# A fused attention and two-MLP kernel: a renewed cost list and a new table of places for the planned order

## The chip, the cores and the metric

The kernel runs on one core of a Trainium2 chip. The metric is the device time of one execution in microseconds (us), from the median of a few runs. A core has five engines that run side by side and meet only through semaphores: TensorE (PE in the profile; its weight loads are PEld), VectorE (DVE), ScalarE (ACT), GpSimd (POOL) and SyncE (SP), which here issues nearly all DMAs.

## The reference, cut to what matters

```python
def _attn_ref(q, k, v, g_q, g_k):            # q, k, v: 4 batches x 12 heads x 448 x 64
    q_n, k_n = rmsnorm(q, g_q), rmsnorm(k, g_k)
    scores = scale * np.matmul(q_n, k_n.transpose(0, 1, 3, 2))
    attn = softmax(scores)                   # with the row maximum taken off
    return np.matmul(attn, v)
x = attn_out.transpose(0, 2, 1, 3).reshape(1792, 768)
def _moe_ref(x, w_in, w_out, g_ln):          # 768 -> 1024 -> 768
    h = x @ w_in
    return layernorm(h * softmax(h)) * g_ln @ w_out
def _moe2_ref(x, w_in, w_out):               # 768 -> 2048 -> 768
    h = x @ w_in
    return (h - np.tanh(h)) @ w_out
```

## The kernel before

The work falls into three parts. Attention runs over 24 pairs of heads, numbered 0 to 23. For a pair the rows of `k` and `q` are loaded (`qk`), normalised (`qn`, on GpSimd from the third pair on), and transposed on TensorE (`qkps`, 4 + 4 small matmuls). ScalarE and VectorE split the result into a high and a low part (`wk`, `wq`), and DMAs on SP's queue spread these over the buffers `k0` to `k2` and `q0` to `q2` ("q<-wq", "k<-wk"). Seven matmuls (`mps`) then give scores whose row maxima VectorE takes (`nm`); a transpose (`nmps`), a copy on ScalarE (`nt`) and a 2 KB DMA ("q<-nt") put the maxima into the `q` buffer, so that the second scores (`sps`, 16 matmuls for a pair) come out with the maximum already taken off. ScalarE takes the exponential (`pf`), and eight matmuls with the values (`pvps`) make the output, which goes through DRAM (`xd`).

The first MLP works on four blocks of tokens and lies between the pairs of the later batches: `hps` (first product), `lps` (transposes of the normalised `hb`), `x2ps` (second product). Its weights are 8-byte numbers in memory: a raw block is loaded (`raw`), turned into floats by a chain on GpSimd or ScalarE and VectorE (`val`), split (`w`), saved to DRAM and read again for later blocks ("w<-w_in", "w<-w_out"). The last block's first product (`moe_h_last`, `hps` with 512 columns) and the second MLP (`h2ps`, `ops`) come last.

What sets the order: a `Recorder` takes down every operation of attention and of the first three blocks' stages with what it depends on, and `place` then simulates the engines. `cost` gives the time that an operation holds its engine and how much later its result is there; `transfer` that of a DMA's data. At each step the earliest engine takes, among the operations that could start, the one with the smallest place: its number in the recording (`op.at`) plus a shift by kind (`op.late`), which `SHIFT` names, for instance "qkps tensor" for transposes on TensorE or "raw load" for loads from the kernel's inputs. `can` says from when an operation may start with regard to buffers. `slack` and `doubt` are added to what comes from another engine and from a DMA, and `ahead` is how long before its first user's start a load may be issued. Where the simulated TensorE would idle, `fill` puts matmuls on a constant tile (`idle<-still`, called fillers below) into the order. The result is issued as it stands, so each engine works through its list in order and waits on semaphores where the simulation was too hopeful. What is recorded after `rec.give()` (the last block's stage and the second MLP) is ordered by the framework, not by this planner.

All operations are issued from one helper, so that the profile puts nearly everything on L203 (L204 in the changed kernel); rows are told apart by their tiles.

Of the kernel before, what the change touches and what calls it, by code (L numbers as in the profile page):

```python
# [167 lines left out]
def _real(x):  # L168
# [1 line left out]


SHIFT = {
    "bs vector": 288, "e scalar": 299, "gln scalar": 64, "gps tensor": -190, "grow vector": 30, "hb scalar": 8,
    "hb vector": 158, "hps tensor": -30, "k scalar": 355, "k vector": -282, "mps tensor": -35, "mv vector": 34,
    "nmps tensor": -256, "nr scalar": 31, "nr vector": -3, "nt scalar": 3, "ones vector": 47, "pf scalar": -23,
    "pvps tensor": 100, "q gpsimd": 9, "q scalar": -94, "q vector": 391, "qd scalar": 405, "qd vector": -111,
    "qk load": -26, "qkps tensor": -1088, "qn gpsimd": 38, "qn vector": -7, "raw load": -69, "rr scalar": 36,
    "rr vector": -247, "rs gpsimd": 6, "rs vector": 91, "sps tensor": -77, "ss vector": 66, "sx scalar": 46,
    "sx vector": -33, "va gpsimd": 84, "va load": -55, "val scalar": -18, "val vector": -10, "w gpsimd": -85,
    "w scalar": 352, "w sync": -115, "w vector": 466, "w_in_ sync": -148, "w_out_ sync": 47, "wk scalar": -155,  # L180
    "wk vector": -42, "wq vector": 123, "x scalar": -55, "x2ps tensor": 314, "xd sync": 13, "xo scalar": -69,
    "xo vector": -16, "xs scalar": 359, "xu vector": -308, "zero vector": -400,
}


class Recorder:
# [51 lines left out]
    def cost(self, op):  # L238
        n = 1
        for d in (op.out.shape if isinstance(op.out, View) else [1, 1])[1:]:  # L240
            n *= d
        src = next((x for x in op.ins if isinstance(x, View)), None)
        m = n
        if src is not None:
            m = 1
            for d in src.shape[1:]:
                m *= d
        big = max(n, m)
        if op.queue == "tensor":
            if op.what == "transpose":  # L250
                return (0.095 if n < 128 else 0.108), 0.2
            rhs = op.kw["rhs"]
            if rhs.root.dtype != F32:
                return 0.0025 + n * 0.000451, 0.2
            return (0.475 if rhs.p1 - rhs.p0 == 64 else 0.75), 0.2
        if op.eng == "dma":
            inside = all(isinstance(x, View) and not x.root.far for x in (op.out, op.ins[0]))
            return (0.62 if inside else 0.46), 0.0
        if op.queue == "scalar":
            t = 0.15 + 0.000875 * big  # L260
            if n <= 64:
                t += 0.045
            t += 0.09 * sum(isinstance(op.kw.get(x), View) for x in ("bias", "scale"))
            if "accum_out" in op.kw:
                t += 0.2
            return t, 0.034
        if op.queue == "gpsimd":
            if op.what == "memset":
                return 0.5, 0.034
            if n == 1:  # L270
                return 0.67, 0.034
            if op.what == "tensor_copy":
                return 0.6, 0.034
            if op.what == "tensor_scalar":
                return 1.6, 0.034
            return (0.25 + 0.0022 * n if op.out.p1 - op.out.p0 == 128 else 1.135), 0.034
        if op.what == "memset":
            return 0.06, 0.034
        if op.what == "tensor_scalar" and n >= 64:
            return 0.2 + 0.00054 * n, 0.034  # L280
        if big <= 16:
            return 0.18, 0.034
        slow = isinstance(src, View) and src.dims and abs(src.dims[-1][0]) > 1
        return 0.156 + 0.00103 * big + (0.1 if slow else 0.0), 0.034

    @staticmethod
    def transfer(op):
        v = op.out if isinstance(op.out, View) else op.ins[0]
        o = next((x for x in op.ins if isinstance(x, View)), v)
        run, size = None, 1  # L290
        for x in (v, o):
            r = 1
            for stride, k in reversed(x.dims):
                if k == 1:
                    continue
                if stride != r:
                    break
                r *= k
            run = r if run is None else min(run, r)
        for d in v.shape:  # L300
            size *= d
        run = 4 * min(run, 512 if len(v.shape) == 4 and v.shape[-1] == 2 else 1024)
        packets = -(-4 * size // run)
        if run < 64:
            return 0.025 * packets
        return max(1, packets / 16.0) * (8 + 0.05 * run) * 1e-3
# [11 lines left out]
    def place(self):  # L318
# [23 lines left out]
        feeds = [[] for _ in ops]  # L342
        for op in ops:
            if op.queue == "tensor":
                r = op.out.root
                for d, o in op.deps.items():
                    if r not in o.refs:
                        r.wait += 1
                        feeds[d].append(r)
            else:  # L350
                for r in op.refs:
                    if r.psum:
                        r.into += [x for x in op.refs if x is not r and x.tile_ is None and not x.psum and x not in r.into]
        opened = dict.fromkeys(queue, 0)
# [8 lines left out]

        def can(op):
            t = op.ready
            for r in op.refs:
                if r.tile_ is not None or r.open:
                    continue
                s = slots[r.key]
                if not s:  # L370
                    return None
                if opened[r.line] != r.turn or r.wait:
                    return None
                t = max(t, r.from_)
                for x in r.into:
                    if not x.open and len(slots[x.key]) < x.turn - opened[x.line] + 1:
                        return None
                if r.psum and r.rank and key_limit.get(r.pool.name, 0) >= len(s):
                    return None
                t = max(t, min(s))  # L380
            return t

        key_limit = self.reserve
# [1 line left out]
        while placed < total:  # L385
# [33 lines left out]
            if op.eng == "dma":  # L419
# [1 line left out]
                    start = max(start, lanes[-8])  # L421
                free[e] = start + took
                wire = max(free[e] + 0.4, wire) + self.transfer(op)
                done = wire + 1.3
                lanes.append(max(done, lanes[-1] if lanes else 0.0))
            else:
                free[e] = start + took
                done = free[e] + late
            op.start, op.done = start, done
            ready[e].remove(op)  # L430
            order.append(op)
# [11 lines left out]
            for u in users[op.at]:  # L443
# [2 lines left out]
                    slack = self.slack[u.rank] + (self.doubt if op.eng == "dma" else 0.0)  # L446
                    u.ready = max(u.ready, done + self.notice.get(u.queue, 0.0) + slack)
                else:
                    u.ready = max(u.ready, start + took)
                if u.left == 0:  # L450
                    ready[u.queue].append(u)
        return order
# [20 lines left out]
    notice = {"tensor": 0.02, "gpsimd": 0.045}  # L473
    lag = 0
    warm = 9.0
    passes, ahead = 2, 12.0
    slack, doubt = (0.0, 0.6), 0.6
    still = None

    def give(self):  # L480
# [888 lines left out]
```

## Time and profile before

| | us |
|---|---|
| median of 3 runs | 1104.23 |
| lowest and highest | 1103.9, 1302.5 |
| the profiled execution | 1106.91 |
| its span, first to last instruction | 1104.9 |
| PE busy in the span | 1075.6 |
| of that in fillers | 50.57 |
| DVE, ACT, POOL busy | 704.2, 495.8, 231.5 |

The profiled execution's own time stands 2.0 us above its span, and 2.7 us above the median. Busy time of PE counts fillers too, and a matmul's recorded length overlaps the next one's, so a busy PE is not yet one that does useful work all the time.

### The profile page before, as it was taken

To read this page: it belongs to the slowest core of one execution; us is meant where nothing else is said; L and a number is where in the kernel's file an instruction comes from. 1 tells how busy PE (TensorE), PEld (TensorE's weight loads), DVE (VectorE), ACT (ScalarE), POOL (GpSimd) and SP (SyncE) were. 2 spreads that over 40 slices of the span, in tenths; PEclk is the share of its full clock that TensorE was granted. 3 is DMA by queue.
4 is the path that set the end of the run, shared out by engine and by line. 5 is a ranking of instruction groups with operands and counts; after the bars stand their busy time and mean duration, and the time that the engine had idled before them with its cause. 6 is when DMAs were issued, how large, how long until landed. Compare 5 with 4: busy or idle time off the path is not lost.

```text
span 1104.9 us, 15904 instructions
## 1 busy us (share of the span) xinstructions
PE 1075.6 (97%) x5716; PEld 906.2 (82%) x5716; DVE 704.2 (64%) x1312; ACT 495.8 (45%) x996; POOL 231.5 (21%) x204
## 2 busy tenths in 40 slices
PE   8898999999999899999899999999999999999998
PEld 7565677757777779779699989899999999998998
DVE  8786767878878843545664057375767666675444
ACT  5675767878667564574154154322212121212110
POOL 2222132302001210003300034242314241422000
PEclk9998999999999999999899999999999999999999
DMA  6886988986999998558586442021111111110004
GB/s 168 201 216 156 255 223 258 255 194 161 277 287 290 309 259 218 185 168 265 171 280 211 152 161 87 32 68 47 58 39 58 58 58 58 58 58 1 1 29 171
DMA packets 112470, 171.21 MB, mean 155 GB/s; under 512 B 30656, under 2 KB 78216, under 8 KB 112392
## 3 DMA queue, kind: packets, MB, share of 16 engines
q1 hardware_dynamic: 112368, 170.20, 53.5%
q8 instruction: 45, 0.74, 0.3%
q14 instruction: 33, 0.27, 0.1%
q10 hardware_dynamic: 24, 0.01, 0.0%
HBM read 109.32 MB, written 29.10 MB: 125 GB/s over the span
## 4 chain that ended last, share of the span: by engine, by line
PE 78%; DMA 10%; DVE 6%; ACT 4%; issue 2%; POOL 1%; SPq 0%; DVEq 0%; ACTq 0%; POOLq 0%
PE ops L203 21%; PE h2ps L203 21%; PE pvps L203 9%; PE x2ps L203 8%; PE hps L203 8%; PE sps L203 5%; PE mps L203 3%; PE idle L203 2%; DMA q<-wq 2%; DVE val L203 2%; DMA w_out<-w 1%; DMA q<-nt 1%; DMA raw<-in_moe_w_out_dram 1%; DMA xr<-xd 1%; PE qkps L203 1%
## 5 line engine op out<-in xcount | busy, mean ns | idle before, releaser
L203 PE MATMUL ops<-w,gT 128*128 128x384 f32 x1344 | 257.6, 336 | 0.0
L203 PE MATMUL h2ps<-x2s,w 128*128 128x512 f32 (+1 forms) x1152 | 256.5, 365 | 0.0
L203 PEld LDWEIGHTS ops<-w,gT 128*128 128x128 f32 x1344 | 235.8, 188 | 8.3
L203 PEld LDWEIGHTS h2ps<-x2s,w 128*128 128x128 f32 x1152 | 200.4, 188 | 27.6
L203 DVE SCALAR_TENSOR_TENSOR val<-raw,val 128x512 int32<-128x512 int32 (+1 forms) x192 | 149.2, 779 | 66.8 <-POOL val L203 63.5
L203 DVE TENSOR_TENSOR ob<-ops,ob 128x384 f32<-128x384 f32 x196 | 108.4, 553 | 102.4 <-PE ops L203 101.9
L203 PE MATMUL pvps<-pf,va 128*128 128x448 f32 (+1 forms) x384 | 172.4, 574 | 0.0
L203 POOL TENSOR_TENSOR w<-val,w 128x512 fp32r<-128x512 f32 x60 | 81.0, 1352 | 389.4 <-ACT w L203 387.0
L203 PE MATMUL sps<-q,k 128*128 128x448 f32 (+3 forms) x400 | 140.1, 457 | 6.2 <-DMA q<-nt 3.7
L203 DVE TENSOR_REDUCE nm<-mps 128x1 f32<-128x448 f32 x168 | 99.4, 618 | 62.2 <-PE mps L203 61.8
L203 PE MATMUL hps<-w,xs 128*128 128x256 f32 (+1 forms) x828 | 132.5, 314 | 4.8 <-ACT hb L203 4.2
L203 PEld LDWEIGHTS hps<-w,xs 128*128 128x128 f32 x828 | 118.1, 193 | 16.2 <-ACT hb L203 4.6
L203 PE MATMUL x2ps<-lnT,w 128*128 128x384 f32 (+1 forms) x720 | 125.3, 329 | 0.3 <-DVE lnT L203 0.3
L203 PEld LDWEIGHTS x2ps<-lnT,w 128*128 128x128 f32 x720 | 117.4, 189 | 5.2 <-issue 3.9
L203 ACT ACTIVATE th<-h2ps 128x512 f32<-128x512 f32 (+1 forms) x64 | 34.8, 544 | 179.6 <-PE h2ps L203 155.7
L203 ACT ACTIVATE pf<-sps 128x448 f32<-128x448 f32 (+1 forms) x169 | 89.1, 539 | 52.7 <-PE sps L203 50.4
L203 PEld LDWEIGHTS sps<-q,k 128*128 128x128 f32 (+3 forms) x400 | 69.6, 186 | 51.8 <-issue 28.1
L203 PEld LDWEIGHTS pvps<-pf,va 128*128 128x128 f32 (+1 forms) x384 | 64.0, 194 | 34.0 <-issue 24.7
L203 POOL TENSOR_SCALAR val<-raw 128x512 f32<-128x512 f32 x48 | 79.0, 1646 | 36.5 <-DVE w L203 17.7
L203 ACT ACTIVATE gT<-th 128x512 fp32r<-128x512 f32 (+1 forms) x64 | 37.1, 579 | 99.1 <-PE ops L203 66.8
L203 POOL TENSOR_TENSOR qn<-qk,rr 112x512 f32<-112x512 f32 x44 | 47.0, 1087 | 144.2 <-DVE rr L203 56.4
L203 DVE TENSOR_TENSOR th<-h2ps,th 128x512 f32<-128x512 f32 (+1 forms) x64 | 39.7, 621 | 44.0 <-ACT th L203 43.9
(95 smaller groups left out, 1036.6 us busy)
## 6 DMA issues: line engine op xcount, KB each, us to landing
w<-w_out SPq DMA_DIRECT2D x48, 512.0 KB
raw<-in_moe_w_in_dram SPq DMA_DIRECT2D x36, 512.0 KB
raw<-in_moe_w_out_dram SPq DMA_DIRECT2D x36, 512.0 KB
w<-w_in SPq DMA_DIRECT2D x24, 512.0 KB
k<-wk SPq DMA_DIRECT2D x46, 224.0 KB
q<-wq SPq DMA_DIRECT2D x46, 224.0 KB
w_in<-w SPq DMA_DIRECT2D x12, 512.0 KB
w_out<-w SPq DMA_DIRECT2D x12, 512.0 KB
```

What stands on the lines that cost most here:

```text
L203: return f(*[_real(x) for x in a], **{n: _real(x) for n, x in kw.items()})
```

## The change

Three things change, all inside the planner. No operation of the computation is added, removed or altered, and the number of instructions on DVE, ACT, POOL and SP stays the same.

The cost list is renewed: a DMA takes SP 0.5, 0.66 or 0.7 us instead of 0.46 or 0.62; its data lands 2.0 us after the wire is done instead of 1.3; a full-precision matmul over 64 rows holds PE 0.58 instead of 0.475 us; VectorE, ScalarE and GpSimd are free 0.08, 0.08 and 0.05 us before an operation ends (`overlap`), but an operation of the same engine that needs the result waits for its end and the delay behind it. The margins are other ones: `slack` by rank (attention, MLP stage) from (0.0, 0.6) to (0.07, 0.18), `doubt` from 0.6 to 0.44, `ahead` from 12 to 185.2 us. The rule for buffers (`can`) now counts an operation that opens several buffers of one kind, and a PSUM buffer waits for the inputs of every matmul that touches it. And the table of places is new in nearly all its entries.

```diff
 SHIFT = {
...
-    "qk load": -26, "qkps tensor": -1088, "qn gpsimd": 38, "qn vector": -7, "raw load": -69, "rr scalar": 36,
+    "nt scalar": -1395, "ones vector": -357, "pf scalar": -1312, "pvps tensor": 76, "q gpsimd": -80, "q scalar": -59,
...
-            return (0.475 if rhs.p1 - rhs.p0 == 64 else 0.75), 0.2
+            return (0.58 if rhs.p1 - rhs.p0 == 64 else 0.75), 0.2
...
-            return (0.62 if inside else 0.46), 0.0
+            return (0.7 if inside else 0.66 if self.run(op)[0] <= 64 else 0.5), 0.0
...
-                r = op.out.root
-                for d, o in op.deps.items():
-                    if r not in o.refs:
-                        r.wait += 1
-                        feeds[d].append(r)
+                for r in op.refs:
+                    for d, o in op.deps.items():
+                        if r.psum and r not in o.refs:
+                            r.wait += 1
+                            feeds[d].append(r)
...
-                if not s:
+                n, m = new.get(r.key, 0), lines.get(r.line, 0)
+                new[r.key], lines[r.line] = n + 1, m + 1
+                if len(s) <= n:
                     return None
-                if opened[r.line] != r.turn or r.wait:
+                if opened[r.line] + m != r.turn or r.wait:
                     return None
...
-                t = max(t, min(s))
+                t = max(t, sorted(s)[n])
...
-                done = wire + 1.3
+                done = wire + 2.0
...
-                free[e] = start + took
-                done = free[e] + late
+                free[e] = start + took - self.overlap.get(e, 0.0)
+                done = start + took + late
...
-                    u.ready = max(u.ready, start + took)
+                    u.ready = max(u.ready, start + took + (0.0 if e == "tensor" else late))
...
-    passes, ahead = 2, 12.0
-    slack, doubt = (0.0, 0.6), 0.6
+    passes, ahead = 2, 185.2
+    overlap = {"vector": 0.08, "scalar": 0.08, "gpsimd": 0.05}
+    slack, doubt = (0.07, 0.18), 0.44
```

What it makes of the order on PE: every matmul of the computation is still there, as often as before, and the rows from the end of the last block's first product to the program's end are the same ones. The fillers go from 183 to 88. Up to the first `pvps` they are 54 before and 50 now; from there to the first `pvps` of pair 8, 44 and 16; to that of pair 13, 8 and 4; to that of pair 18, 72 and 10; behind it 5 and 8.

The first place is on PE in the first half of attention, in pairs 5 to 7. A row is one instruction or several equal ones. Before:

```order
L203 MATMUL sps<-q_183,k_177 128x448
L203 MATMUL sps<-q_183,k_177 64x448 x2
L203 MATMUL mps<-k_165,q_173 128x448
L203 MATMUL idle<-still 128x128 x2
L203 MATMUL mps<-k_165,q_173 128x448 x2
L203 MATMUL idle<-still 128x128 x6
L203 MATMUL mps<-wk,qd_155 128x448
L203 MATMUL qkps<-idf,qn 128x112 x4
L203 MATMUL pvps<-pf,va 128x448
```

Now, at the same step of a pair:

```order
L204 MATMUL sps<-q_173,k_159 128x448 x2
L204 MATMUL sps<-q_173,k_159 64x448 x2
L204 MATMUL mps<-wk,qd_152 128x448
L204 MATMUL qkps<-idf,qn 128x112 x8
L204 MATMUL mps<-k_178,q_161 128x448 x3
L204 MATMUL idle<-still 128x128
L204 MATMUL mps<-k_178,q_161 128x448
L204 MATMUL pvps<-pf,va 128x448 x2
```

Both transposes of a pair (`qkps` x8) now stand together, the first three maxima of the next pair follow them, and value matmuls (`pvps`) are kept back to follow; eight fillers there have become one.

The second place is on PE where the second product of the first block begins, in pairs 16 to 18. Before:

```order
L203 MATMUL idle<-still 128x128 x8
L203 MATMUL x2ps<-lnT,w_3922 128x384
L203 MATMUL mps<-k_185,q_161 128x448
L203 MATMUL x2ps<-lnT,w_3922 128x384 x5
L203 MATMUL mps<-k_185,q_161 128x448
L203 MATMUL x2ps<-lnT,w_3922 128x384 x6
L203 MATMUL x2ps<-lnT,w_3927 128x384 x12
L203 MATMUL mps<-wk,qd_157 128x448
L203 MATMUL idle<-still 128x128 x6
L203 MATMUL nmps<-idf,nm 4x128
L203 MATMUL idle<-still 128x128 x21
L203 MATMUL pvps<-pf,va 128x448
```

Now:

```order
L204 MATMUL pvps<-pf,va 128x448 x2
L204 MATMUL mps<-k_178,q_161 128x448 x2
L204 MATMUL x2ps<-lnT,w_3794 128x384 x3
L204 MATMUL mps<-wk,qd_183 128x448
L204 MATMUL x2ps<-lnT,w_3794 128x384 x6
L204 MATMUL nmps<-idf,nm 4x128
L204 MATMUL x2ps<-lnT,w_3794 128x384 x3
L204 MATMUL x2ps<-lnT,w_3800 128x384 x3
L204 MATMUL sps<-q_180,k_170 128x448 x6
L204 MATMUL x2ps<-lnT,w_3800 128x384
L204 MATMUL sps<-q_180,k_170 128x448 x2
```

The products `x2ps` are dealt out among the maxima and scores, and the 35 fillers of the piece before are gone.

The third place is on DVE behind the planned part, in the last block's first product: `val` is the conversion of the second MLP's weights (the number of its `raw` block tells which), `mx` the maximum that reads `hps` out of PSUM. Before:

```order
L203 SCALAR_TENSOR_TENSOR val<-raw_5836,val 128x512
L203 TENSOR_SCALAR val<-val 128x512
L203 TENSOR_REDUCE mx<-hps 128x1
L203 SCALAR_TENSOR_TENSOR val<-raw_5836,val 128x512
L203 SCALAR_TENSOR_TENSOR val<-raw_5846,val 128x512
L203 TENSOR_REDUCE mx<-hps 128x1 x2
```

Now:

```order
L204 SCALAR_TENSOR_TENSOR val<-raw_5734,val 128x512
L204 TENSOR_SCALAR val<-val 128x512
L204 SCALAR_TENSOR_TENSOR val<-raw_5734,val 128x512
L204 TENSOR_REDUCE mx<-hps 128x1
L204 SCALAR_TENSOR_TENSOR val<-raw_5734,val 128x512
L204 TENSOR_REDUCE mx<-hps 128x1 x3
```

Before, the first maximum stood behind the second operation of the fifth conversion; now it stands behind the third operation of the sixth.

## Rows read from the trace of the kernel before

**Rows 1.** The page's head: span, and PE's busy time, share and count.

```profile
span 1104.9 us, 15904 instructions
...
PE 1075.6 (97%) x5716; PEld 906.2 (82%) x5716; DVE 704.2 (64%) x1312; ACT 495.8 (45%) x996; POOL 231.5 (21%) x204
```

**Rows 2.** Busy time by stretch (us), granted clock, DMA share, GB/s.

```profile
core 0: us, PE busy (x) PEld busy (x) DVE busy (x) ACT busy (x) POOL busy (x), PEclk, DMA share, GB/s
...
25.00:150.00 125.00, 117.07 (x499) 74.44 (x497) 94.89 (x168) 89.50 (x190) 28.54 (x30) 0.95 0.81 204
150.00:275.00 125.00, 122.48 (x663) 91.44 (x662) 92.12 (x186) 95.45 (x199) 28.56 (x31) 1.00 0.85 222
275.00:400.00 125.00, 118.93 (x646) 93.30 (x646) 100.49 (x216) 82.46 (x189) 18.17 (x21) 0.97 1.01 288
...
510.00:545.00 35.00, 30.79 (x136) 25.03 (x135) 25.74 (x36) 10.78 (x19) 14.52 (x11) 0.90 0.72 235
545.00:1105.00 560.00, 555.67 (x3041) 515.36 (x3039) 320.28 (x560) 145.44 (x252) 123.78 (x86) 1.00 0.26 85
```

**Rows 3.** The same for fillers alone (two records each): one stretch, whole span.

```profile
275.00:400.00 125.00, 14.23 (x115) 13.90 (x114) 0.97 1.01 288
...
sum 1105.00, PE 50.57 PEld 48.11; mean PE 7.22 PEld 6.87
```

**Rows 4.** Pieces of the chain that ended last: start us, us, what.

```profile
32.70 5.55 DMA q<-nt
...
349.20 4.69 PE idle L203 x42
...
374.69 8.36 DMA q<-nt
```

**Rows 5.** PE's longest waits to 510 us: total us, times, longest us.

```profile
PE sps L203 <- DMA q<-nt: 3.7, 2, 1.9
PE mps L203 <- DMA q<-wq: 2.8, 3, 2.0
PE mps L203 <- DVE wk L203: 2.1, 1, 2.1
```

**Rows 6.** Busy time by stretch, four stretches at half the clock.

```profile
38.80:42.20 3.40, 3.40 (x7) 1.74 (x6) 0.93 (x3) 1.72 (x4) 0.00 (x0) 0.50 0.83 207
...
90.00:100.20 10.20, 10.20 (x19) 4.99 (x19) 2.13 (x5) 2.90 (x8) 0.00 (x0) 0.50 0.38 114
...
383.60:387.00 3.40, 3.40 (x9) 2.16 (x7) 3.06 (x11) 2.64 (x6) 1.57 (x2) 0.50 1.02 327
...
537.20:544.00 6.80, 6.04 (x14) 4.79 (x15) 6.41 (x11) 3.59 (x6) 1.47 (x3) 0.50 0.59 200
```

**Rows 7.** Instructions in order of time, 340 to 356 us: start, us, engine, what.

```profile
341.94 0.52 ACT L203 ACTIVATE pf<-sps 128x448 f32<-128x448 f32 x1
...
349.04 4.85 PE L203 MATMUL idle<-still 128*128 128x128 f32 x42
...
353.73 0.92 PE L203 MATMUL pvps<-pf,va 128*128 128x448 f32 x2
```

**Rows 8.** The same around 236 us on PE, idle time before in brackets.

```profile
233.94 1.07 PE L203 MATMUL idle<-still 128*128 128x128 f32 x8
237.14 0.64 PE L203 MATMUL mps<-k,q 128*128 128x448 f32 x2 [2.13 <-DVE wk L203]
```

**Rows 9.** The same around 536 us, on DVE.

```profile
535.22 0.69 DVE L203 SCALAR_TENSOR_TENSOR val<-raw,val 128x512 f32<-128x512 f32 x1 [3.55 <-POOL val L203]
...
536.60 0.68 DVE L203 TENSOR_REDUCE mx<-hps 128x1 f32<-128x512 f32 x1
```

**Rows 10.** The same on PE.

```profile
537.96 3.35 PE L203 MATMUL hps<-w,xs 128*128 128x512 f32 x7 [4.21 <-ACT hb L203]
```

**Rows 11.** The same around 516 us, on DVE.

```profile
515.81 0.68 DVE L203 TENSOR_TENSOR lnT<-lps,lnT 128x512 fp32r<-128x512 f32 x1
516.41 0.68 DVE L203 SCALAR_TENSOR_TENSOR val<-raw,val 128x512 int32<-128x512 int32 x1
```

More of the change, by code (lines that the diff above doesn't have):

```diff
@@ L172 @@
 SHIFT = {
[L173 to L176, printed above, removed]
-    "qk load": -26, "qkps tensor": -1088, "qn gpsimd": 38, "qn vector": -7, "raw load": -69, "rr scalar": 36,
[L178 to L182, printed above, removed]
+    "bs vector": 61, "e scalar": 372, "gam scalar": 54, "gln scalar": -176, "glr load": -133, "grow load": 127,
+    "hb scalar": 709, "hb vector": 727, "hps tensor": -61, "k scalar": 33, "k vector": -511, "lnT scalar": -27,
+    "lnT vector": -468, "mv vector": -324, "nm vector": -5, "nmps tensor": -112, "nr scalar": 647, "nr vector": -428,
+    "nt scalar": -1395, "ones vector": -357, "pf scalar": -1312, "pvps tensor": 76, "q gpsimd": -80, "q scalar": -59,
+    "q sync": 43, "q vector": -148, "qd scalar": -121, "qd vector": 197, "qk load": 123, "qkps tensor": -1541,
+    "qn gpsimd": -22, "qn vector": 18, "raw load": 176, "rr scalar": 128, "rr vector": 326, "rs gpsimd": 177,
+    "rs vector": 7, "sm vector": 63, "sps tensor": 3, "sq scalar": 1359, "ss vector": 194, "sx scalar": -14,
+    "va load": 108, "val scalar": 231, "val vector": -44, "w gpsimd": 21, "w scalar": -36, "w sync": 77,
+    "w vector": -244, "w_in_ sync": -91, "w_out_ sync": 19, "wk scalar": 565, "wk vector": 5, "wq scalar": 1978,
+    "x scalar": 22, "x2ps tensor": 312, "xd sync": 40, "xo scalar": 69, "xo vector": -253, "xr sync": -60,
+    "xs scalar": 16, "xs vector": -126, "xu scalar": 232, "xu vector": 7, "zero vector": -3,
 }
@@ L286, in transfer, with run @@
     @staticmethod
-    def transfer(op):
+    def run(op):
         v = op.out if isinstance(op.out, View) else op.ins[0]
@@ L301, in transfer @@
             size *= d
-        run = 4 * min(run, 512 if len(v.shape) == 4 and v.shape[-1] == 2 else 1024)
+        return min(run, 512 if len(v.shape) == 4 and v.shape[-1] == 2 else 1024), size
+    def transfer(self, op):
+        run, size = self.run(op)
+        run *= 4
         packets = -(-4 * size // run)
@@ L365, in can @@
             t = op.ready
+            new, lines = {}, {}
             for r in op.refs:
```

## The prediction

> **What bounds the kernel now.** I read the page's head first: PE is busy for 1075.6 of 1104.9 us [rows 1], so the time is what PE has to do, plus what keeps it from doing so. The second view, busy time by stretch, tells where that is. From 545 us on PE is busy for 555.67 of 560 us at the full clock, with DMA at a quarter of its share [rows 2]; that is the stretch behind the planner, and its order is the same now. Up to 400 us all is close together: in 275 to 400 us PE has 118.93, DVE 100.49 and ACT 82.46 of 125 us, and the DMA engines are taken for their whole share, 1.01 [rows 2]. So the change can only act on the first 510 us or so, and a little beyond by what it hands over.
>
> The third view is that of the fillers alone. They make 50.57 us of PE's busy time, all of it in the planned part [rows 3]. The reader should see that this is idle time that looks like work. Their busy time overlaps what follows; what a filler keeps PE is better read from the chain, where 42 records (two for each filler, so 21 of them) take 4.69 us: 0.223 us each [rows 4]. All 183 then make 40.8 us.
>
> The fourth is PE's own waits. The three longest groups up to 510 us are waits for landings and for the split of the transposes, 3.7, 2.8 and 2.1 us, mostly in single waits of 1.9 to 2.1 us [rows 5]. Behind three of these the granted clock is 0.50, which is the lower of its two levels, 1.2 GHz, for 3.4, 10.2 and 3.4 us; a fourth such stretch of 6.8 us follows the wait of 4.21 us at 537.96 us [rows 6, 10]. At half the clock half of the work of a stretch is lost, so that the first three cost about 1.7 + 5.1 + 1.7 = 8.5 us more, as much as the waits themselves.
>
> **The change, part by part.** The work itself: every matmul stays, and each costs what it did. Its parts on DVE, ACT, POOL and SP keep their number too, so these edits cost nothing as instructions; only the places move.
>
> The fillers: 95 fewer, at 0.223 us, are 21.2 us [rows 4]. Where they go: 28 in pairs 0 to 7, up to about 150 us, 62 in pairs 13 to 17, and a net 5 elsewhere. The bounds: a filler that went was worth nothing if PE waits in its place, and all of it if the next matmul has its data. The trace has both. At 349.04 us the run of 21 holds back a `pvps` whose exponential was over at 342.46 us, and the `pvps` starts without idle time when they end [rows 7]: needless. At 233.94 us the next `mps` had to wait for 2.13 us more behind four of them [rows 8]: that gap was real, even too small. But a real gap in one order is not one in another: in both places that front shows on PE, `pvps`, `sps` or `x2ps` whose inputs come from other pairs or blocks stand where the fillers stood. I take the whole 21.2 us for the sum, nearer to the run of 21, and keep half of it as the lower end of what they bring.
>
> Why the new plan can do with less: the old list let a VectorE operation on 512 elements hold its engine for 0.68 us. Two such operations, each 0.68 us long, start 0.60 us apart [rows 11], so with DVE busy for 80% of the stretch of 275 to 400 us the old plan saw it too late by 0.08 us for each operation, and put fillers where PE had to wait only in the plan. The new overlap of 0.08 us is what these rows show.
>
> The landings: a transfer now lands 2.0 + 0.44 us behind the wire in the plan instead of 1.3 + 0.6, 0.54 us later, so that its users move back. The two "q<-nt" on the chain took 5.55 and 8.36 us from issue to landing [rows 4], and by the code the plan allows about 3.5 us now, 2.9 before. So the plan is still too hopeful, but less so. Against that stands the smaller margin for the MLP's stages, 0.18 instead of 0.6 us. At best the 8.6 us of the three groups and the 8.5 us of slow clock go, together 17.1 us; at worst as much again is added. I take a third of the gain, 5.5 us, since 0.54 us is a quarter of a wait of 2 us and a shorter wait may leave the clock alone.
>
> The Trainium skill, DMA: Bandwidth & Descriptors, "Anatomy of one DMA", gives a fixed cost of about 2.0 us for a transfer, nearly constant, most of it the wait for the receipt. By it the new landings would be right and all 17.1 us would come. The two rows of 5.55 and 8.36 us for 2 KB differ from it: here a small transfer stands behind others.
>
> The loads: `ahead` lets a load of `qk`, `va` or `raw` be issued as soon as its buffer is free, no longer only 12 us ahead. The bytes are the same. The cover is the wire's spare share before 275 us, 0.81 and 0.85 [rows 2]; without it each load that waits for its buffer at the head of SP's queue holds up the "q<-wq" and "q<-nt" queued behind it, for which PE waits. I take nothing for it in the sum; its price is in the rivals.
>
> What is handed over: in the last block's first product PE waited for 4.21 us, since the first maximum on DVE, at 536.60 us, stood behind the fifth conversion [rows 9, 10]. Now it stands behind the sixth, five operations later, at 0.60 us [rows 11] 3.0 us. If the conversions start earlier by that much, nothing changes. No row shows which; I take the middle, 1.5 us more, with 0 and 3.0 as ends.
>
> The sum: -21.2 - 5.5 + 1.5 = -25.2 us. The profiled execution of 1106.9 us (span 1104.9) becomes 1081.7; the median lies 2.7 us lower, at 1104.2, so the forecast is 1079.0 us.
>
> **The rivals.** First, the stretch from 275 to 400 us is set by transfers, and gaps elsewhere come back as waits. For it: the share of 1.01 [rows 2], and a "q<-nt" that took 8.36 us there [rows 4]. Against it: PE had 14.23 us of fillers there [rows 3], with runs that nobody needed [rows 7]. 57 fillers lie there (115 records [rows 3]) and by the order 13 now in the same pairs, 44 of the 95 or 9.8 us, and half of the other 51 is 5.7 us. With both the time is 1079.0 + 15.5 = 1094.5, with the first alone 1088.8; I put 1092.
>
> Second, the waits go as well. With the 17.1 us in place of 5.5 the time is 1067.4, and without the wait of 4.21 us and its slow clock (3.4 us) instead of 1.5 us more, 1058.3. For it: longer planned landings. Against it: they are still shorter than the rows.
>
> Third, slower: with fewer fillers PE has less in hand when a landing is late, and eager loads make landings late. The place is the first `mps` or `sps` of a pair behind "q<-wq" or "q<-nt". The price is a wait of 2.0 us and 1.7 us of slow clock, as at 38.8 us, 3.7 us together, or 7.1 us as at 90.0 us [rows 5, 6]. Seven of the small ones eat the gain (25.2 / 3.7), and thirteen in the 24 pairs give 1079.0 + 48.1 = 1127.1, slower by over 2%. Against it: with fillers before the landings too, only two or three such waits came in 24 pairs [rows 5].
>
> On that price the Trainium skill, TensorE: Matmul & The Clock Gate, "HAM oscillation", says that an array which waits for DMA is put back to the low clock and that each such wait is paid for again. The trace agrees in three waits of about 2 us [rows 6]; after the one at 237.14 us the clock in the stretch stays 1.00 [rows 2, 8]. By that rule every new wait would cost the larger price, and seven would be enough for 1127.
>
> Fourth, that the order changes and the time doesn't is left little room: it needs the same 25.2 us of new waits by chance.
>
> **How the numbers follow.** The forecast has 0.52, and its own range is 1070 to 1089 (the landings' term and the hand-over between their ends, the fillers within a fifth). The waits going as well has 0.22, the transfers' bound and gaps that return 0.18, new waits 0.08. The range of 1061 to 1095 leaves out most of the last (0.08), a little of the third and the lower part of the second, together less than 0.2. Two per cent, about what a measurement of this kernel can tell from no change, is 22.1 us: below 1082.1 is faster, above 1126.3 slower. Of the forecast's own range about 0.63 lies below 1082.1, 0.33 of chance, and all of the 0.22: faster 0.55. Slower is most of the last, 0.06, and the rest, 0.39, is within.
>
> **What the profile afterwards would show.** Fillers: about 176 records, 20 to 25 us busy, and PE's stretch to 545 us shorter by about 25 us with the rest at the same 560. Landings: PE's waits for "q<-nt" and "q<-wq" at or below 6.5 us together, and less than 17 us at half the clock before 510 us. Hand-over: the wait for `hb` in the last block's first product between 4 and 7 us. I am wrong if the fillers fall as the order says and the waits of PE grow by as much: then the gaps were the computation's, not the plan's. I am wrong on the transfers if the stretch at a DMA share of 1.0 is as long as it was.

## The result, and the profile after

The changed kernel takes 1067.72 us (median of four runs, 1065.89 to 1069.34) against 1104.31 for the kernel before. The ratio is 0.9661, with a 95% interval of 0.9632 to 0.9690: faster, by 36.6 us. One execution of the kernel before, of 1302.5 us, was far slower than the others and does not enter the ratio. The forecast was 1079.0 us, so the direction and the range hold, and the gain is 11 us larger than the likeliest case. The profiled execution is that of 1065.89 us, and its span stands 41.1 us below that of [rows 1].

The head of the page, to be read against [rows 1]:

```profile
span 1063.8 us, 15536 instructions
...
PE 1038.2 (98%) x5526; PEld 880.2 (83%) x5526; DVE 692.4 (65%) x1312; ACT 493.2 (46%) x996; POOL 235.0 (22%) x204
```

PE has 190 records fewer, two for each of 95 fillers; the counts of DVE, ACT and POOL are what they were. Busy time by stretch, with the columns of [rows 2]:

```profile
25.00:150.00 125.00, 120.78 (x562) 81.92 (x561) 98.60 (x186) 100.29 (x214) 36.12 (x39) 1.00 0.92 237
150.00:275.00 125.00, 123.86 (x665) 92.14 (x664) 105.38 (x221) 100.26 (x223) 25.82 (x29) 0.99 0.95 263
275.00:400.00 125.00, 120.25 (x675) 96.74 (x674) 87.74 (x185) 82.48 (x183) 17.85 (x18) 1.00 0.98 285
...
504.00:1064.00 560.00, 554.54 (x3036) 514.19 (x3034) 317.70 (x556) 145.41 (x252) 123.57 (x85) 1.00 0.26 83
```

The tail of 560 us is the same. All of the gain lies ahead of it. In 275 to 400 us PE's busy time has hardly grown, but less of it is fillers, as the same view for fillers alone shows against [rows 3]:

```profile
275.00:400.00 125.00, 3.38 (x26) 3.36 (x26) 1.00 0.98 285
```

So PE does 116.9 us of work there instead of 104.7, at no higher share of the DMA engines. The planned part ends where the last block's first transposes (`lps` on `hb`) start on PE. That row in the trace of the kernel before:

```profile
510.31 1.03 PE L203 MATMUL lps<-idf,hb 128*128 128x128 f32 x8
```

And after:

```profile
469.63 1.03 PE L204 MATMUL lps<-idf,hb 128*128 128x128 f32 x8
```

The planned part is 40.7 us shorter; from there to the end it is 594.6 us before and 594.2 now. PE's waits in the planned part (us in total, times, longest), to be read against [rows 5]:

```profile
PE sps L204 <- ACT pf L204: 4.1, 2, 2.5
PE sps L204 <- DVE nm L204: 1.8, 2, 1.5
PE nmps L204 <- DVE nm L204: 1.7, 1, 1.7
PE hps L204 <- DMA w<-w_in: 1.3, 1, 1.3
PE mps L204 <- DMA q<-wq: 1.3, 2, 0.7
...
PE sps L204 <- DMA q<-nt: 0.4, 1, 0.4
```

The waits for landings, 6.5 us before, are 1.7 us, and all of this view's groups together fall from 20.1 to 15.6 us. Only two stretches are left at half the clock, one of them in the planned part:

```profile
148.80:152.20 3.40, 3.40 (x12) 3.08 (x13) 3.39 (x5) 0.91 (x2) 1.27 (x1) 0.50 1.04 353
497.00:500.40 3.40, 3.33 (x8) 2.68 (x9) 3.37 (x7) 2.19 (x5) 0.15 (x1) 0.50 0.62 186
```

The first follows a wait for an exponential (start us, us, idle time before in brackets):

```profile
148.70 1.06 PE L204 MATMUL sps<-q,k 128*128 128x448 f32 x2 [2.47 <-ACT pf L204]
```

Before, the planned part had the three of [rows 6] and a fourth that the prediction had not listed:

```profile
311.90:315.30 3.40, 3.40 (x7) 1.81 (x7) 2.79 (x5) 1.68 (x5) 0.00 (x0) 0.50 0.95 340
```

That is 20.4 us at half the clock before and 3.4 now, or 8.5 us of lost work. The account of the 40.7 us: 95 fillers at 0.223 us make 21.2, listed waits 4.5, the clock 8.5, together 34.2. The other 6.5 us are not idle time, as PE's busy time in the planned part shows, before and after:

```profile
0.00:510.31 510.31, 489.43 (x2544) 366.08 (x2545) 358.52 (x717) 339.60 (x725) 93.41 (x109) 0.98 0.83 227
```

```profile
0.00:469.63 469.63, 453.28 (x2354) 341.24 (x2355) 348.57 (x720) 336.94 (x726) 96.00 (x109) 1.00 0.89 246
```

Without a matmul are 20.9 us before and 16.4 now, so that gaps too short for the list of waits make 0.8 us in both. The 6.5 us lie in matmuls that follow one another sooner at the full clock, mainly in the second scores: from the start of a record of `sps` with 128x448 to the next start it takes 0.310 us before and 0.288 now on the mean, 322 times (worked out from the starts in the two traces). Why is not shown.

This account is of two single executions, and executions of one kernel differ in their clock. Over the 52 executions of the kernel before that stand beside the later runs, the mean granted clock (as a share of full speed) goes from 0.986 to 0.998, and the time falls with it from 1110.84 to 1095.12 us; the straight line that fits them best falls by 1.05 us for each 0.001. The profiled execution before has 0.987, near the low end; the one after has 0.997, the upper end of its four (0.993 to 0.997). At 0.997 the kernel before took 1098.20 to 1099.99 us (four executions) and the changed one 1065.89 and 1066.39, so some 33 of the 36.6 us do not hang on the clock. The 8.5 us of the two traces are therefore more than the clock is worth in the medians.

### The profile page after: what moved, and what is told of

The parts are those of the page before. It is cut to its first block, busy times and chain, and to the rows that moved or that the text cites. A ratio compares the mean times of both kernels' runs of the same rounds, so it can differ in the third digit from the quotient of the medians.

```text
span 1063.8 us, 15536 instructions
## 1 busy us (share of the span) xinstructions
PE 1038.2 (98%) x5526; PEld 880.2 (83%) x5526; DVE 692.4 (65%) x1312; ACT 493.2 (46%) x996; POOL 235.0 (22%) x204
## 4 chain that ended last, share of the span: by engine, by line
PE 77%; DMA 9%; DVE 6%; ACT 3%; issue 2%; SPq 1%; POOL 1%; ACTq 0%; DVEq 0%; POOLq 0%
PE ops L204 22%; PE h2ps L204 22%; PE x2ps L204 9%; PE pvps L204 8%; PE hps L204 6%; PE sps L204 5%; PE mps L204 2%; DMA raw<-in_moe_w_in_dram 2%; DMA xr<-xd 2%; DVE val L204 2%; DMA w<-w_in 1%; DVE nm L204 1%; PE qkps L204 1%; SPq L204 1%; PE idle L204 1%
## 5 line engine op out<-in xcount | busy, mean ns | idle before, releaser
L204 PE MATMUL pvps<-pf,va 128*128 128x448 f32 (+1 forms) x384 | 158.5, 555 | 0.0
L204 PE MATMUL sps<-q,k 128*128 128x448 f32 (+2 forms) x400 | 130.5, 432 | 6.8 <-ACT pf L204 4.1
L204 PEld LDWEIGHTS sps<-q,k 128*128 128x128 f32 (+2 forms) x400 | 69.2, 183 | 45.3 <-issue 17.8
L204 PEld LDWEIGHTS pvps<-pf,va 128*128 128x128 f32 (+1 forms) x384 | 61.1, 188 | 37.5 <-issue 33.9
L204 POOL TENSOR_TENSOR qn<-qk,rr 112x512 f32<-112x512 f32 x44 | 50.4, 1163 | 116.9 <-DVE rr L204 54.0
```

What stands on the lines that cost most here:

```text
L204: return f(*[_real(x) for x in a], **{n: _real(x) for n, x in kw.items()})
```

## Experiments

**Were the fillers needless?** The prediction read the run of 21 at 349.04 us [rows 7] as time given away. Three kernels take fillers out and leave the order of everything else alone. In the first two `fill` puts nothing into the order:

```
-        if n < 1 or not keys:
+        if True:
             return
```

The kernel before without its 183 fillers:

> The kernel before, with the same order but without its 183 fillers; all real work is left in its order. Theory 'needless fillers': in the trace of the kernel before, 18.3 of the 50.5 us in runs of fillers lie where the next matmul already had its data, so leaving all out gives 12 to 18 us back (1086 to 1092 us), and the rest turns into waits of PE of about 25 us. Rival 'fillers keep the clock': the new waits bring more half-clock stretches and the time is the same or longer (1104 to 1125 us). Rival 'every filler is a loss': 183 x 0.223 us = 40.8 us come back, 1063 us.

Measured: 1112.51 us, ratio 1.0073 (1.0043 to 1.0102). It is slower, by 0.7%. The page's head and PE's longest waits in the planned part:

```profile
PE 1048.5 (95%) x5350; PEld 869.1 (78%) x5350; DVE 704.3 (64%) x1312; ACT 495.8 (45%) x996; POOL 231.8 (21%) x204
```

```profile
PE mps L203 <- DVE nm L203: 7.1, 9, 2.2
PE mps L203 <- ACT pf L203: 7.1, 8, 1.8
PE gps L203 <- DVE grow L203: 6.0, 1, 6.0
PE mps L203 <- ACT qd L203: 5.5, 3, 2.7
```

The 40.8 us of fillers come back as waits, which grow from 20.1 to 50.6 us, and as clock: 27.2 us of the planned part are at half the clock instead of 20.4. There is a third part, which the clock's column does not show, since it stands at 1.00 in the first 40 us. Four transposes (`qkps`) with fillers, without them, and in the stretch of the kernel before that is at half the clock from 90.0 us [rows 6]:

```profile
13.08 0.55 PE L203 MATMUL qkps<-idf,qn 112*128 112x112 f32 x4
```

```profile
13.71 1.01 PE L203 MATMUL qkps<-idf,qn 112*128 112x112 f32 x4
```

```profile
92.49 1.01 PE L203 MATMUL qkps<-idf,qn 112*128 112x112 f32 x4
```

Without fillers PE works at that pace for its first 40 us, and the first `pvps` starts at 41.85 us instead of 34.85, 7.0 us later. From there to the `lps` it takes 472.4 us without fillers and 475.5 with them, so the 129 fillers behind the start, 28.8 us by the price of one, held PE up by 3.1 us. Over all ten executions the mean granted clock is 0.987, against 0.992 in the nineteen of the kernel before measured beside them, which is worth 5 to 6 us. The theory of needless fillers falls, and so does the rival that each of them is a loss; that fillers keep the clock is what these numbers bear out.

The changed kernel without its 88 fillers:

> The changed kernel, with the same order but without its 88 fillers. Theory 'needless fillers': 8.3 of the 28.6 us in its runs of fillers lie where the next matmul already had its data, so 4 to 8 us come back, 1060 to 1064 us. Rival 'fillers keep the clock': the same or longer, 1067 to 1080 us, with more than the 6.8 us at half the clock that the changed kernel has.

Measured: 1070.65 us, ratio 0.9715 (0.9669 to 0.9762), against 0.9661 with them: the same within the intervals. The waits grow from 15.6 to 30.7 us; the half clock stays at 6.8 us. Only at the start do these fillers hold it: without them four `qkps` take 1.01 us at 14.82 us, as above, and the first `pvps` starts 1.3 us later (34.98 us instead of 33.67).

The kernel before, with only those fillers left out during which the next matmul already had its data; `KEEP` is the number that each of the 45 runs keeps:

```
+KEEP = [9, 5, 1, 7, 1, 0, 0, 2, 0, 3, 2, 7, 0, 0, 1, 1, 0, 0, 3, 4, 5, 0, 7, 2, 4, 7, 3, 1, 0, 3, 1, 4, 6, 5, 0, 2, 0, 0, 2,
+        0, 7, 6, 0, 4, 1]
...
+        n = self.kept.pop(0) if self.kept else 0
```

> The kernel before with the same order and 116 of its 183 fillers; the 67 that are left out are those during which, in the trace of the kernel before, the next matmul already had its data (the run of 21 at 349 us among them). Theory 'these were needless', as the prediction read that run: 67 x 0.223 = 14.9 us come back, 1089 us (1087 to 1092). Rival 'what a filler holds back is made up by a wait later on', as the run without any filler showed for all 183: 1100 to 1108 us.

Measured: 1103.41 us, ratio 1.0010 (0.9983 to 1.0037): the same. But the clock hides a gain. The mean granted clock of its ten executions is 0.984 to 0.989, that of the thirteen of the kernel before measured beside them 0.990 to 0.998; the means, 0.987 and 0.993, are some 7 us apart at 1.05 us for each 0.001. The two profiled executions have the same clock, 0.987, and there the planned part is 5.4 us shorter (504.88 instead of 510.31 us). So the 67 fillers held PE up by 5 to 7 of the 14.9 us, and the clock took that back. What becomes of the run of 21 is seen on PE. In the trace of the kernel before, PE stands ahead of the run and after the pair's scores as follows (start us, us):

```profile
348.93 0.27 PE L203 MATMUL nmps<-idf,nm 128*4 128x128 f32 x1
...
361.49 1.93 PE L203 MATMUL x2ps<-lnT,w 128*128 128x384 f32 x10
```

Without the run:

```profile
344.13 0.27 PE L207 MATMUL nmps<-idf,nm 128*4 128x128 f32 x1
344.24 0.92 PE L207 MATMUL pvps<-pf,va 128*128 128x448 f32 x2
...
350.99 0.47 PE L207 MATMUL sps<-q,k 128*128 128x448 f32 x1 [1.00 <-DMA q<-nt]
352.98 0.60 PE L207 MATMUL qkps<-idf,qn 112*128 112x112 f32 x4 [1.52 <-POOL qn L207]
...
355.65 2.66 PE L207 MATMUL x2ps<-lnT,w 128*128 128x384 f32 x9
```

From `nmps` to the first `x2ps` it takes 12.56 us with the run and 11.52 without it. The `pvps` does start 4.7 us sooner, as the prediction read it, but 3.6 of the 4.7 us are gone within 12 us: scores then wait 1.00 us for their maxima and transposes 1.52 us for GpSimd, and from 354.2 us on the clock is at half. Most of what this run of fillers held back, the next links of the chain were not ready for.

**Table or costs?** For what follows one more number helps, which is no measurement: the planner works out when its last planned matmul starts. The trace tells when it did; it is 0.2 us ahead of the `lps` shown above. The difference is what the chip adds to the plan. The old table of places with the new costs, and the new table with the old costs, where the diff is the table of the change in one direction or the other:

> The changed kernel with the old table of places, so the new costs, margins and buffer rules alone; its order holds 141 fillers, 42 fewer than before. If the costs by themselves bring the gain: 1068 to 1075 us. If only the fillers that they take out count: 42 x 0.223 = 9.4 us, 1095 us (1088 to 1100). If table and costs belong together: 1104 us or more.

Measured: 1081.47 us, ratio 0.9797 (0.9753 to 0.9841).

> The kernel before with the new table of places and everything else as before; its order holds 194 fillers. If the table by itself brings the gain: 1068 to 1075 us. If it is only good together with the new costs (my theory, since the fillers stay): 1095 to 1115 us.

Measured: 1101.96 us, ratio 0.9971 (0.9945 to 0.9996). The new costs alone bring about 22 us, with a table that was not made for them; the new table alone brings next to nothing; the table on top of the new costs brings the other 15. The reason shows in the two parts of the time (us, one profiled execution each, up to 5 us from the median of its kernel):

| kernel | planned | measured | added by the chip | of the measured at half clock | fillers |
|---|---|---|---|---|---|
| before | 457.8 | 510.1 | 52.3 | 20.4 | 183 |
| new table, old costs | 465.1 | 507.3 | 42.2 | 17.0 | 194 |
| old table, new costs | 454.3 | 488.3 | 34.0 | 3.4 | 141 |
| changed | 439.8 | 469.5 | 29.7 | 3.4 | 88 |
| changed, old landing | 446.5 | 487.3 | 40.8 | 6.8 | 114 |
| changed, no overlap | 475.5 | 497.5 | 22.0 | 3.4 | 230 |
| changed, loads 12 us ahead | 449.6 | 484.1 | 34.5 | 13.6 | 123 |
| changed, one place altered by 1 | 450.7 | 485.1 | 34.4 | 10.2 | 130 |
| changed, landing 3.0 us | 455.9 | 491.8 | 35.9 | 10.2 | 158 |

Of the 40.6 us, 18.0 are a shorter plan and 22.6 are less that the chip adds to it. With the old table the new costs take 18.3 us off what is added; with the new costs the new table takes 14.5 us off the plan. Under the old costs the new table makes the plan longer, by 7.3 us.

Two parts of the 22.6 us are no better plan. The two executions differ by 17.0 us at half the clock, which is 8.5 us. And the two lists price the same work differently: the 48 value matmuls over 64 rows (96 records of `pvps`, two for each) cost 0.105 us more each in the new list, so that 5.0 us stand in its plan and not in what is added. That leaves 9.1 of the 22.6 us, and 4.8 of the 18.3 us, which is no more than single executions differ by. The medians show that the new costs bring 22 us with the old table; they do not show that this is because the plan comes nearer to the chip.

**What is one part of the cost list worth?** Three parts undone in the changed kernel, one at a time. Each was measured beside the kernel before, and what it costs against the changed kernel is the difference of the two ratios. The landing:

```
-                done = wire + 2.0
+                done = wire + 1.3
...
-    slack, doubt = (0.07, 0.18), 0.44
+    slack, doubt = (0.07, 0.18), 0.6
```

> The changed kernel with the old landing in its cost list (1.3 us behind the wire, doubt 0.6); all else as changed; its order holds 114 fillers. Theory 'the landings took PE's waits and the slow clock away', as the prediction has it: PE's waits for q<-nt and q<-wq come back to about 6.5 us from 1.7, half clock before 510 us to 10 us or more from 6.8, and the time rises by 6 to 17 us, 1074 to 1085. Rival 'the table and the other costs did': waits at 1 to 3 us, and 1066 to 1073 us.

Measured: 1085.38 us, ratio 0.9842 (0.9799 to 0.9885), about 20 us more than the changed kernel. The chip adds 11.1 us more to this plan, but not where theory had it. Waits of PE for a DMA in the planned part:

```profile
PE hps L204 <- DMA w<-w_in: 2.0, 1, 2.0
PE mps L204 <- DMA q<-wq: 1.0, 1, 1.0
```

The waits for "q<-nt" and "q<-wq" did not come back (1.0 us together), and before 510 us there are 6.8 us at half the clock, not 10, so the theory's mechanism falls, though the time lies at the upper end of what it gave. The 11.1 us are only in part found: all listed waits together grow by 4.1 us, to 19.7, and the half clock in the planned part by 3.4 us, worth 1.7. The other 5.3 us stay open.

The overlap, and the loads:

```
-    overlap = {"vector": 0.08, "scalar": 0.08, "gpsimd": 0.05}
+    overlap = {}
```

> The changed kernel without the overlap of 0.08, 0.08 and 0.05 us of VectorE, ScalarE and GpSimd in its cost list; its order holds 230 fillers. Theory of the prediction, 'the old list saw VectorE too late, and put fillers where PE waited only in the plan': the order is much like the changed one and the 142 more fillers hold it back in part, 10 to 30 us, 1078 to 1098. Rival 'a filler only fills a gap that is there': the time follows the order's own gaps, 1066 to 1075 us.

Measured: 1089.52 us, ratio 0.9873 (0.9833 to 0.9914). Fillers alone, whole planned part:

```profile
0.00:500.00 500.00, 62.66 (x460) 60.28 (x460) 1.00 0.84 233
```

With engines that the plan holds too long, the plan is 35.7 us longer and full of fillers, and the chip adds only 22.0 us to it, the least of all. The time is as the first theory had it, but its reason isn't: the order is another one, and the fillers in it were not shown to hold anything back. Its time from the `lps` to the end is 588.4 us, 5.8 less than in the changed kernel: there the first maximum of the hand-over starts 22.7 us behind the `lps` instead of 26.1, and PE's wait for the copy is 0.7 us.

```
-    passes, ahead = 2, 185.2
+    passes, ahead = 2, 12.0
```

> The changed kernel with loads issued at most 12 us ahead of their first user, as before, in place of 185.2; its order holds 123 fillers. The prediction took 0 for this: 1065 to 1070 us. If the eager loads carry a part of the gain: 1073 us or more, with longer landings of loads in front of PE's waits.

Measured: 1081.31 us, ratio 0.9813 (0.9764 to 0.9862), 17 us more than the changed kernel.

Three unlike parts, each worth 17 to 23 us, are more than the whole gain. So a control: one number of the table altered so that it means nothing.

```
-    "nt scalar": -1395, "ones vector": -357, "pf scalar": -1312, "pvps tensor": 76, "q gpsimd": -80, "q scalar": -59,
+    "nt scalar": -1395, "ones vector": -357, "pf scalar": -1312, "pvps tensor": 77, "q gpsimd": -80, "q scalar": -59,
```

> The changed kernel with one number of the table altered by one place (pvps tensor 77 for 76), which means nothing for any cost. Its plan, worked out by the planner, puts the last planned matmul's start at 450.7 us instead of 439.8 and holds 130 fillers. Theory 'the time is the plan's own length plus what the chip adds to it' (in the changed kernel 469.5 measured against 439.8 planned, 29.7 us more): 11 us more than the changed kernel, 1079 us (1075 to 1084), as much as undoing a part of the cost list cost. Rival 'each part of the cost list is worth its own 15 to 23 us': a number that means nothing costs nothing, 1066 to 1070 us.

Measured: 1080.35 us, ratio 0.9792 (0.9765 to 0.9819), about 14 us more. That is as much as the loads or the whole old table cost. The table fits one plan, that of 439.8 us; in every variant of the changed kernel in which the planner chose otherwise, the plan is 7 to 36 us longer and the time 14 to 23. What a part of the list costs when it is undone therefore says little of the part.

The same control in the direction that the prediction called too hopeful:

```
-                done = wire + 2.0
+                done = wire + 3.0
```

> The changed kernel with landings 3.0 us behind the wire in the cost list instead of 2.0; its plan puts the last planned matmul's start at 455.9 us and holds 158 fillers. Theory 'plan's length plus what the chip adds': longer landings take 0 to 8 us off the 29.7 us that the chip adds, so that the planned part ends at 478 to 486 us and the time is 1076 to 1085. Rival, the prediction's reading that the plan was still too hopeful of landings and that later ones only take waits away: below 1066 us.

Measured: 1080.54 us, ratio 0.9787 (0.9754 to 0.9819), within the first theory's time; but the planned part ended at 491.8 us, not at 478 to 486, so in the profiled execution, the slowest of its four, what the chip adds did not fall. The rival is out: later landings do not make this kernel faster.

And the landing alone, in the kernel before:

```
-                done = wire + 1.3
+                done = wire + 2.0
...
-    slack, doubt = (0.0, 0.6), 0.6
+    slack, doubt = (0.0, 0.6), 0.44
```

> The kernel before with the new landing alone (2.0 us behind the wire instead of 1.3, doubt 0.44 instead of 0.6); old table, all other costs as before. Its plan puts the last planned matmul's start at 464.4 us (before: 457.8, measured 510.1) and holds 212 fillers. Theory 'a truer landing takes about 11 us off what the chip adds to the plan', as its removal from the changed kernel put 11.1 us on (40.8 for 29.7): measured at about 505 us, and 1096 to 1102 us in all, with PE's waits for q<-nt and q<-wq down from 6.5 us to 3 or less. Rival 'what the chip adds has other causes': 52 us again, 516 us, and 1106 to 1112 us in all.

Measured: 1101.87 us, ratio 0.9959 (0.9928 to 0.9990), 4.5 us less than before and within the theory's time, with a plan that is 6.6 us longer. But the mean granted clock is 0.995 in its other nine executions and 0.990 in the thirteen of the kernel before measured beside them, worth about 5 us, as much as the whole difference. So the run does not show that the landing takes anything off what the chip adds; whether the new landing raised the clock stays open. Its profiled execution took 1112.63 us, 10.8 above its median, so its waits are not read.

**The hand-over.** PE's longest wait is still there (start us, us, idle time before in brackets), to be read against [rows 9, 10]:

```profile
492.83 1.77 DVE L204 SCALAR_TENSOR_TENSOR val<-raw,val 128x512 f32<-128x512 f32 x1 [1.42 <-POOL val L204]
...
495.70 0.68 DVE L204 TENSOR_REDUCE mx<-hps 128x1 f32<-128x512 f32 x1
...
496.42 0.60 ACT L204 ACTIVATE hb<-hps 128x512 f32<-128x512 f32 x1 [4.35 <-DVE mx L204]
...
497.07 5.24 PE L204 MATMUL hps<-w,xs 128*128 128x512 f32 x15 [4.02 <-ACT hb L204]
```

PE waits for the copy, the copy for the maximum, and the maximum stands behind a conversion on DVE. If the maximum reads the copy instead, PE needs only ScalarE:

```
+                        part = hb[:, 512 * r:512 * r + 512]
+                        copy(nc.scalar, out=part, in_=ps[u])
                         nc.vector.tensor_reduce(
-                            out=mx_t[b][:, u, r:r + 1], in_=ps[u], axis=AX.X, op=ALU.max, negate=True
+                            out=mx_t[b][:, u, r:r + 1], in_=part, axis=AX.X, op=ALU.max, negate=True
                         )
-                        copy(nc.scalar, out=hb[:, 512 * r:512 * r + 512], in_=ps[u])
```

> The changed kernel, where in the last block's first product ScalarE's copy stands before VectorE's maximum and the maximum reads the copy instead of PSUM; the same operations, in the same number. If PE's wait of 4.0 us at 497 us hangs on the first maximum standing behind the conversions on VectorE, as the prediction read it, the wait falls to about 1 us and the 3.4 us at half clock behind it go: 3 to 5 us less than the changed kernel, 1063 to 1065 us, wait and clock in the trace. Rival 'the copies or the maxima are late further on': the wait comes back behind the first product, 1067 to 1070 us.

Measured: 1062.99 us, ratio 0.9632 (0.9606 to 0.9659), the fastest of all, though its interval and that of the changed kernel (0.9632 to 0.9690) overlap. The trace bears out the cause:

```profile
469.88 1.03 PE L204 MATMUL lps<-idf,hb 128*128 128x128 f32 x8
...
483.80 16.54 PE L204 MATMUL hps<-w,xs 128*128 128x512 f32 x72
...
491.90 2.53 ACT L204 ACTIVATE hb<-hps 128x512 f32<-128x512 f32 x5
```

72 records of `hps` run without a wait, there is no half clock behind them, and from the `lps` to the end it takes 588.3 us (span 1058.2) instead of 594.2: 5.9 us less, the wait of 4.0 and 1.7 of slow clock.

## Why the prediction was right, and where it was not

**What bounds the kernel, and where.** Right. The tail of 560 us is the same, and the whole gain lies in the planned part.

**The fillers, -21.2 us.** The size is right (95 at 0.223 us, and no new waits took their place), but the reason given is not. The step that failed is "the old plan saw it too late by 0.08 us for each operation, and put fillers where PE had to wait only in the plan". Without any fillers the old order is slower by 0.7%. Without the needless ones its planned part is 5.4 us shorter at the same clock, about a third of the 14.9 us that they took, and its median is the same: most of the gaps were the order's own, and the run of 21 that the prediction called needless was mostly made up for within 12 us. What went is idle time in the order, of which fillers are the measure. That a gap of one order need not be one of another, the other reason that stood there, is what held.

**The landings, -5.5 us.** This is the term that was mis-sized. A third of 17.1 us was taken. Between the two profiled executions the three groups of waits fell from 8.6 to 1.7 us, and the half clock in the planned part by 17.0 us, worth 8.5: 15.4 us of the 17.1 came, against which other waits grew by 2.4 us. Part of that is the choice of the execution, since only some 3 us of the medians' 36.6 hang on the clock. Another 6.5 us, in matmuls that follow one another sooner, stood in no term. The reason for taking a third, that 0.54 us is a quarter of a wait, treated the landing as the only thing that acts on a landing's wait. It is not: with the old landing in the changed kernel the waits for "q<-nt" and "q<-wq" are 1.0 us, with the new costs and the old table 0.6, with the old costs and the new table 4.5, before 6.5. So the waits went with the list as a whole, and not with the landing's figure. Which entries did it could not be told apart, since undoing any of them moves the whole plan. By the Trainium skill, DMA: Bandwidth & Descriptors, "Anatomy of one DMA", and its fixed cost of about 2.0 us all 17.1 us were to come. That sum came nearer, but not shown to be for that reason: the page gives the figure for transfers that GpSimd issues, those here are issued on SP's queue, and with the old landing in the plan the waits stayed away too.

**The loads, 0.** Not shown either way: undoing it costs 17 us, hardly more than the number that means nothing.

**The hand-over, +1.5 us.** What the wait hangs on was right, as the maximum taken from the copy shows, and the size was not. The wait is 4.02 us instead of 4.21, the slow stretch behind it 3.4 us instead of 6.8, and from the `lps` to the end it takes 0.4 us less. The first maximum starts 26.1 us behind the `lps` now and 26.3 before: the conversions start earlier by as much as the maximum stands later, the lower end of the term.

**The rivals.** The second, that the waits go as well, is what happened; its 1067.4 us had 0.22. That it is met within 0.4 us is luck: the clock gave the medians less than its 8.5 us, and the 6.5 us that it did not have made up for that. The first, transfers as the bound, is refuted: at a share of 0.98 the stretch of 275 to 400 us holds 12.2 us more work. The third, new waits behind landings, did not come: 1.7 us for the two landings together. For the clock behind a wait the trace has both sides again: half behind the waits of 2.47 us at 148.70 and 4.02 at 497.07, full behind the single ones of 1.5 (`sps` for `nm`) and 1.7 us (`nmps`). The prediction took the Trainium skill, TensorE: Matmul & The Clock Gate, "HAM oscillation", to mean that every new wait is paid for again; the page tells it of a kernel whose waits for DMA are longer, and here the short ones were not paid for.

## What to carry to other kernels

Fillers that a planner writes measure the idle time of its order; taking them out gains little unless the order can use the time, so price them by what the next links of the chain are ready for, not by the next instruction alone, and look at the granted clock of all executions before calling the result nothing. The time of a planned part can be split into the plan's own length and what the chip adds, but two plans compare only by the same prices, and the clock of the one profiled execution has to come off first. Before a part of such a list is given credit, alter a number that means nothing, and see what that costs.

## What the runs showed of the hardware that was not expected

The time of one and the same kernel follows its mean granted clock closely: 52 executions of the kernel before lie between 0.986 with 1110.84 us and 0.998 with 1095.12 us, on a line of 1.05 us for each 0.001. So a median can hide a gain that the clock takes back, as with the 67 fillers, or show one that is the clock's, as perhaps with the landing alone.

Leaving out 88 fillers in the changed kernel, with its waits of PE rising from 15.6 to 30.7 us in total, left the stretches that the profile shows at half the clock as they were, 6.8 us, and behind its start a tensor engine that idles in pieces of 1 to 2 us mostly kept its clock. In the kernel before it did not: leaving out 183 lowered the mean granted clock from 0.992 to 0.987, leaving out 67 from 0.993 to 0.987. And without fillers PE's first matmuls ran at the pace of half the clock, for 40 us in the kernel before and 28 in the changed one, while the profile's clock stood at 1.00.
